# Block-sparse attention and a leaky MLP in one kernel: the weights' sign from ScalarE's multiplication, attention in bursts of four units, new priorities

## The chip, the core and the metric

The kernel runs on one core of a Trainium2 chip. The metric is the device time of one execution in microseconds; a smaller one is better. TensorE (PE in the profile) multiplies matrices, VectorE (DVE), ScalarE (ACT) and GpSimd (POOL) do elementwise work, and SyncE (SP) issues the loads and stores.

## The reference

Four sequences of 768 positions with 8 heads of 64 go through attention in which a query sees the keys less than 16 positions away and the 24 block summaries of its head (maximum of keys, mean of values, over blocks of 32). The result, 3072 rows of 512, goes through two matrix products with a leaky step between them:

```
k_sum = k.reshape(B, H, nb, 32, D).max(axis=3); v_sum = v.reshape(B, H, nb, 32, D).mean(axis=3)
scores_l = where(|pos_q - pos_k| < 16, scale * q @ k.T, -1e9);  scores_s = scale * q @ k_sum.T + log(32)
a = softmax(concat(scores_l, scores_s));  x = a @ concat(v, v_sum)      # then heads side by side
h = x @ w_in;  g = maximum(0.01 * h, h);  out = g @ w_out               # (3072,512) (512,2048) (2048,512)
```

## The kernel before

**The MLP.** The rows are cut into 8 chunks of 384 (`T`), and the 2048 middle columns into 16 steps `f` of 128. Each operand is split into a high and a low part in fp32r, and a product is three: high by high, high by low, low by high. For a chunk and a step, `m1` puts 12 matmuls of 384 columns into a PSUM tile `h` (an "h block"); ScalarE makes `ghi` and `gs` from it (L538, L535), the leaky step in high part and in full; VectorE subtracts them to `glo` (L541); `m2` adds 9 matmuls of 512 columns (an "a block", L550 to L552) into three accumulators. An a block stands behind the h block of the next step. The order of the parts is chunk 0 with the first `SPL` steps, chunk 1 with all, the rest of chunk 0, and then chunk by chunk, so that the weights may come in little by little.

**Weights.** w_in and w_out stay in SBUF. `weights(f, w, t)` prepares a block of 128 by 512 for each step and matrix, 32 in all. The words arrive as float64 (`raw`, in a ring of 6 buffers tagged "big"), each as two 32-bit words, and are put together to float32: s0 shifts the low word right by 29 (VectorE, L485), s1 copies the sign as a 16-bit mask from the high word (VectorE, L489), s2 multiplies the high word, read as a float32, by 2^-112, which moves the exponent (ScalarE, L492), s3 shifts it left by 3 and joins the two (VectorE, L495), s4 makes the high part (ScalarE, L498), s5 the low part by subtraction (VectorE, L501).

**Attention.** A unit is 128 queries of a pair of heads, 12 units to a chunk, 96 in all. `pair(m)` handles two units in three pieces on TensorE: "s" (scores, L323, 8 matmuls that the trace shows as 16 rows), "t" (4 transposes of the normalized exponentials, L340), and "o" (values, L346, 8 matmuls, 16 rows). Between s and t VectorE takes mask and maximum (L328), ScalarE the exponential (L335), VectorE the norm (L408, L412, L416); between t and o ScalarE copies the transposes (`pt`, L426); behind o ScalarE and VectorE write x in two parts (L435, L438). From chunk 1 on, `group` joins the scores of one pair, the values of the second pair before it and the transposes of the one between them to a group on TensorE, which stands among the MLP's blocks.

**What sets the order.** Every operation is given to a list scheduler (`Plan`) with an engine, a cost and a priority; `order` runs through a model of the engines, the load queue and the buffers and writes down a fixed order for each engine. The constants at the head of the file (`PLACE`, `OFF`, `LOADS`, `PL`, `WT` and others) are priorities in units of attention. On TensorE, "spare" matmuls on zeros (L639) are put in up to the first h block where the plan expects it to wait.

Of the kernel before, what the change touches and what calls it, by code (L numbers as in the profile page):

```python
# [8 lines left out]
F32 = mybir.dt.float32  # L9
# [15 lines left out]
LK = 120  # L25
TPC = 3
# [16 lines left out]
PL = -1.087
WS = 0.974
WS2 = 1.452
LD = 4.616
XP = 0.547
VT = 2.875
KP = -0.231
KS = -2.395  # L50
XW = -1.124
B1 = 6
USQ = 0.579
WT = 3.757
W0 = 0.79
WO = 1.464
CUT = 3
OFF = {'s': (1.446, 0.604), 'ttr': (-4.554, 0.093), 'ex': (1.991, -0.067), 'nrm': (-1.17, 0.313), 't': (-2.49, -0.132), 'pt': (-3.602, 1.198), 'o': (2.219, -0.005), 'xhi': (0.869, -0.883), 'xlo': (10.088, -1.826)}
LOADS = [('kn', 0, 1), ('q', 0, 0), ('kn', 0, 0), ('q', 0, 1), ('vb', 0, 0), ('mask',), ('vb', 0, 2), ('kn', 0, 2), ('vb', 0, 1), ('kn', 0, 3), ('q', 0, 3), ('q', 0, 2), ('v', 0, 2), ('v', 0, 0), ('v', 0, 1), ('w', 0, 0), ('v', 0, 3), ('w', 1, 0), ('w', 1, 1), ('w', 0, 1)]
# [91 lines left out]
def build(tc, ctx, a):  # L151
# [201 lines left out]
    def group(m, phase, kind, cost, fn, **kw):  # L353
        j = m + "sto".index(kind)
# [24 lines left out]
        return x["op"], g  # L379

    def pair(m):
# [74 lines left out]
        o = pe("t", 600, v1, tr, [("a0", kt, 1)], after=[nm], use=[("e", m)])  # L456
        o = P.op("ACT", ACT(512, True), v1 + 0.3 + off("pt"), pt, after=[o], use=[kt], alloc=[(tag_p, ("pt", m), buf_p)])
        o = pe("o", 600, v2, av, [(ko_tag, ko, 1)], after=[o] + v_op[c, p] + v_op[c, p1], use=[("pt", m)] + kv)
# [8 lines left out]
    def weights(f, w, t):  # L467
# [34 lines left out]
        o = load_op(("w", f, w), t - 0.25 * BIG, load, alloc=[("big", kr, BIG)], size=128 * 4096, rate=290.0)  # L502
        o = P.op("DVE", DVE(512, True), t + 0.05, s0, after=[o], use=[kr], port=True)
# [16 lines left out]
    def mlp(c, f0, f1, t0):  # L520
# [16 lines left out]
        def ghi(f):  # L537
            nc.scalar.activation(out=gnew("ghi", G("ghi", f)), in_=tl[G("h", f)][:, :T], func=AF.Prelu, alpha=0.01)  # L538
# [154 lines left out]
```

## Time and profile before

| | |
|---|---|
| median of three runs | 656.93 us (656.62 to 657.16) |
| span of the profiled execution | 654.36 us; its own time is not listed, and the median lies 2.57 us above the span |
| TensorE busy | 643.2 us (98%), 4613 matmul rows |
| VectorE busy | 280.5 us (43%), nearly all of the first 120 us |
| ScalarE busy | 294.4 us (45%) |
| loads and stores | 58.07 MB |

A row of an engine gives the start and the duration of an instruction in the span. TensorE's instructions overlap and their ends are modelled, so what a block costs is read from its start to the start of what follows.

### The profile page before, as it was taken

Reading aid. Unit: us, or ns where it says so; the run is one execution under the profiler, and the core shown is the slowest. Engines: PE = TensorE matmul, PEld = TensorE weight load, DVE = VectorE, ACT = ScalarE, POOL = GpSimd, SP = SyncE. Lnnn points to the kernel's source line nnn. Section 1 sums busy time; section 2 is a strip of 40 time slices with the busy share of each in tenths; the row PEclk is TensorE's granted clock in tenths of the full one; section 3 lists DMA queues with packets and bytes.
Section 4 is the critical chain, followed back from the end, with each engine's and each line's share of the span. In section 5 each row is a group of like instructions: output and inputs, shape, how many; then the busy total and the mean of one; then the engine's idle time right before and its main releaser. Section 6 shows DMA issues by size and latency. Waiting matters only on the chain.

```text
span 654.4 us, 11674 instructions
## 1 busy us (share of the span) xinstructions
PE 643.2 (98%) x4613; PEld 561.7 (86%) x4613; DVE 280.5 (43%) x907; ACT 294.4 (45%) x874; POOL 6.9 (1%) x18
## 2 busy tenths in 40 slices
PE   8899999999999999999999999999999999999997
PEld 6687788889888888888888898888888988899996
DVE  5899999741475333322534242233223322111111
ACT  4798777353554433534434353354334433222112
POOL 2100000000000000000000000000000000000000
PEclk9999999999999999999999999999999999999999
DMA  8987775500464111121613021121001200010001
GB/s 303 288 251 224 226 233 184 162 26 14 137 189 136 54 43 46 38 72 36 179 51 112 24 72 37 36 83 37 13 24 48 72 1 2 0 50 1 0 1 48
DMA packets 27206, 58.07 MB, mean 89 GB/s; under 512 B 3024, under 2 KB 13328, under 8 KB 27152
## 3 DMA queue, kind: packets, MB, share of 16 engines
q1 hardware_dynamic: 27152, 57.33, 28.7%
q8 instruction: 36, 0.59, 0.4%
q14 instruction: 18, 0.15, 0.1%
HBM read 48.97 MB, written 6.29 MB: 84 GB/s over the span
## 4 chain that ended last, share of the span: by engine, by line
PE 84%; DVE 14%; ACT 1%; issue 1%; ACTq 0%
PE h L531 36%; PE a L552 12%; PE a L551 12%; PE a L550 12%; DVE raw L489 3%; DVE raw L495 2%; DVE win_lo L501 2%; DVE raw L485 1%; DVE wout_lo L501 1%; PE spare L639 1%; DVE glo L541 1%; DVE e L328 1%; DVE e L416 1%; ACT e L335 1%; DVE xl L438 1%
## 5 line engine op out<-in xcount | busy, mean ns | idle before, releaser
L541 DVE TENSOR_TENSOR glo<-gs,ghi 128x384 fp32r<-128x384 f32 x128 | 71.4, 558 | 265.9 <-ACT gs L535 264.0
L531 PE MATMUL h<-xh,win_hi 128*128 128x384 f32 x512 | 175.7, 343 | 0.4 <-ACT win_hi L498 0.4
L538 ACT ACTIVATE ghi<-h 128x384 fp32r<-128x384 f32 x128 | 62.7, 490 | 251.1 <-PE h L531 250.9
L531 PE MATMUL h<-xh,win_lo 128*128 128x384 f32 x512 | 173.6, 339 | 0.3 <-DVE win_lo L501 0.2
L531 PE MATMUL h<-xl,win_hi 128*128 128x384 f32 x512 | 173.2, 338 | 0.0
L552 PE MATMUL a<-wout_hi,glo 128*128 128x512 f32 x384 | 151.7, 395 | 0.9 <-DVE glo L541 0.8
L551 PE MATMUL a<-wout_lo,ghi 128*128 128x512 f32 x384 | 150.8, 393 | 1.5 <-DVE wout_lo L501 1.5
L550 PE MATMUL a<-wout_hi,ghi 128*128 128x512 f32 x384 | 151.8, 395 | 0.0
L531 PEld LDWEIGHTS h<-xh,win_hi 128*128 128x128 f32 x512 | 96.1, 188 | 5.2 <-ACT win_hi L498 1.1
L531 PEld LDWEIGHTS h<-xl,win_hi 128*128 128x128 f32 x512 | 96.4, 188 | 4.4
L531 PEld LDWEIGHTS h<-xh,win_lo 128*128 128x128 f32 x512 | 96.1, 188 | 1.4 <-DVE win_lo L501 1.4
L552 PEld LDWEIGHTS a<-wout_hi,glo 128*128 128x128 f32 x384 | 72.1, 188 | 17.8 <-DVE glo L541 2.5
L551 PEld LDWEIGHTS a<-wout_lo,ghi 128*128 128x128 f32 x384 | 72.2, 188 | 13.8 <-DVE wout_lo L501 2.5
L550 PEld LDWEIGHTS a<-wout_hi,ghi 128*128 128x128 f32 x384 | 72.1, 188 | 11.0 <-issue 0.2
L335 ACT ACTIVATE e<-e,m 128x120 f32<-128x120 f32 x192 | 73.7, 389 | 9.6 <-DVE m L328 9.6
L535 ACT ACTIVATE gs<-h 128x384 f32<-128x384 f32 x128 | 62.3, 487 | 0.2 <-DVE glo L541 0.2
L335 ACT ACTIVATION_READ_ACCUMULATOR e<-e,m 128x1 f32 x192 | 36.7, 191 | 0.0
L416 DVE TENSOR_TENSOR e<-e,z 128x480 f32<-128x480 f32 x48 | 32.1, 669 | 1.3
L492 ACT ACTIVATE raw<-raw 128x512 f32<-128x512 f32 x32 | 21.8, 693 | 10.4 <-DVE raw L489 9.5
L408 DVE TENSOR_SCALAR z<-z 128x4 f32<-128x4 f32 x48 | 8.2, 172 | 36.6 <-ACT e L335 36.5
L489 DVE TENSOR_SCALAR raw<-raw 128x512 int16<-128x512 int16 x32 | 23.4, 766 | 0.0
L495 DVE SCALAR_TENSOR_TENSOR raw<-raw 128x512 int32<-128x512 int32 x32 | 21.6, 694 | 0.0
(588 smaller groups left out, 520.3 us busy)
## 6 DMA issues: line engine op xcount, KB each, us to landing
raw<-in_w_dram SPq DMA_DIRECT2D x32, 512.0 KB
v<-in_v_dram SPq DMA_DIRECT2D x32, 288.0 KB
kn<-in_k_dram SPq DMA_DIRECT2D x16, 400.0 KB
k<-in_q_dram SPq DMA_DIRECT2D x32, 192.0 KB
out_dram<-out SPq DMA_DIRECT2D x21, 256.0 KB
vb<-in_vb_dram SPq DMA_DIRECT2D x12, 384.0 KB
kn<-in_k_dram SPq DMA_DIRECT2D x16, 208.0 KB
v<-vsum SPq DMA_DIRECT2D x24, 72.0 KB
```

The source lines that it names most:

```text
L335: nc.scalar.activation(out=e[:, n], in_=e[:, n], func=AF.Exp, scale=-1.0, bias=m[:, n:n + 1], accum_out=z[:, n:n + 1])
L416: nc.vector.tensor_tensor(out=e, in0=e, in1=z.unsqueeze(2).broadcast_to([128, 4, LK]), op=ALU.mult)
L489: nc.vector.tensor_scalar(out=w16[:, :, 1], in0=w16[:, :, 3], scalar1=-2 ** 15, scalar2=None, op0=ALU.bitwise_and)
L492: nc.scalar.mul(hw(), hw(), 2.0 ** -112)
L495: nc.vector.scalar_tensor_tensor(out=li(), in0=hi_i(), scalar=3, in1=li(), op0=ALU.logical_shift_left, op1=ALU.bitwise_or)
L531: nc.tensor.matmul(h[:, :T], w[:, k, 128 * f:128 * f + 128], x[:, k], start=n == 0, stop=n == 11)
L535: nc.scalar.activation(out=new("gs", G("gs", f), [128, T], bufs=1), in_=tl[G("h", f)][:, :T], func=AF.Prelu, alpha=0.01)
L538: nc.scalar.activation(out=gnew("ghi", G("ghi", f)), in_=tl[G("h", f)][:, :T], func=AF.Prelu, alpha=0.01)
L541: nc.vector.tensor_tensor(out=gnew("glo", G("glo", f)), in0=tl[G("gs", f)], in1=tl[G("ghi", f)].bitcast(F32), op=ALU.subtract)
L550: nc.tensor.matmul(o, gh, wout_hi[:, f], start=f == f0, stop=False)
L551: nc.tensor.matmul(o, gh, wout_lo[:, f], start=False, stop=False)
L552: nc.tensor.matmul(o, gl, wout_hi[:, f], start=False, stop=f == f1 - 1)
```

## The change

Three edits.

1. In `weights`, s1 is taken out. s2 becomes the leaky step `Prelu` with scale 2^-112 and slope 2^32 for negative words: a negative word leaves it with an exponent 32 higher, and behind the shift left by 3 that bit is the sign. s2 follows the load directly and no longer s1; s3 waits for s0 and s2.
2. From chunk 2 on, `quad(q)` replaces `pair(m)`: the scores of four units in one block, with the transposes of a pair before; then the values of the four units before, in one block, with other transposes. x is written in 512 columns at a time. The number and sizes of the matmuls stay. Chunks 0 and 1 keep pairs.
3. The costs of the pieces in the plan and all priorities are set anew; `SPL` is 11 instead of 10, and `CUT`, the number of steps whose h block is cut in two at the start, 1 instead of 3. gs and ghi get priorities of their own, and gs now stands ahead of ghi.

```diff
-        def s1():
-            w16 = tl[kr].bitcast(I16).rearrange("p (n t) -> p n t", t=4)
-            nc.vector.tensor_scalar(out=w16[:, :, 1], in0=w16[:, :, 3], scalar1=-2 ** 15, scalar2=None, op0=ALU.bitwise_and)
-
         def s2():
-            nc.scalar.mul(hw(), hw(), 2.0 ** -112)
+            nc.scalar.activation(out=hw(), in_=hw(), func=AF.Prelu, scale=2.0 ** -112, alpha=2.0 ** 32)
...
-        o = P.op("DVE", DVE(512, True), t + 0.1, s1, after=[o], use=[kr], port=True)
-        o = P.op("ACT", ACT(512), t + 0.1, s2, after=[o], use=[kr])
-        o = P.op("DVE", DVE(512), t + 0.12, s3, after=[o], use=[kr], port=True)
+        o1 = P.op("ACT", ACT(512), t + 0.05, s2, after=[lo_], use=[kr])
+        o = P.op("DVE", DVE(512), t + 0.12, s3, after=[o, o1], use=[kr], port=True)
...
+    def quad(q):
+        us = range(4 * q, 4 * q + 4)
...
+        def qk():
+            for n, u in enumerate(us):
+                scores(u, [tl[ks[0]], tl[ks[1]]], LK * n)
...
+        def av():
+            for n, u in enumerate(us):
+                values(u, tl[ko], 128 * n)
...
+        s_op = group(2 * q, 2, "s", CS4, qk, after=[o for p in hs for o in k_op[c, p]], use=[("k", c, p) for p in hs])[0]
...
+            kt = ("to", ("g", 2 * q + 1 + w, 2))
+            o = group(2 * q + 1 + w, 2, "t", CT, lambda m=m, kt=kt: tr(m, kt), after=o, use=[("e", m)])[0]
...
+        o = group(2 * q + 3, 2, "o", CO4, av, after=pts + [o for p in hs for o in v_op[c, p]], use=[("pt", 2 * q), ("pt", 2 * q + 1)] + [("v", c, p) for p in hs])[0]
...
-    for m in range(NCH * UPC // 2):
+    for m in range(2 * UPC // 2):
         pair(m)
+    for q in range(2 * UPC // 4, NCH * UPC // 4):
+        quad(q)
```

TensorE's order in the even stretch, a group of chunk 6 among the blocks of chunk 5; `s_('g', ...)` is the PSUM tile of scores and values, `to_('g', ...)` that of transposes. Before:

```order
L552 MATMUL a_0_2_4089<-wout_hi,glo_8_4440 128x512
L323 MATMUL s_('g', 36, 2)_4470<-k_0_4265 64x120 x2
L323 MATMUL s_('g', 36, 2)_4471<-k_0_4265 64x120 x2
L323 MATMUL s_('g', 36, 2)_4470<-k_0_4265 64x120 x2
L323 MATMUL s_('g', 36, 2)_4471<-k_0_4265 64x120 x2
L346 MATMUL s_('g', 36, 2)_4470<-pt_4396,v_2_3891 64x64 x4
L346 MATMUL s_('g', 36, 2)_4470<-pt_4396,v_3_4137 64x64 x4
L340 MATMUL to_('g', 36, 2)_4472<-ident,e_4392 120x128 x4
L531 MATMUL h_10_4493<-xh_80,win_hi 128x384
```

In the changed kernel, the group of the same number and the next one:

```order
L610 MATMUL a_0_2_4061<-wout_hi,glo_8_4394 128x512
L323 MATMUL s_('g', 36, 2)_4424<-k_0_4222 64x120 x2
...
L323 MATMUL s_('g', 36, 2)_4425<-k_1_4236 64x120 x2
L340 MATMUL to_('g', 36, 2)_4426<-ident,e_4226 120x128 x4
L589 MATMUL h_10_4447<-xh_80,win_hi 128x384
...
L610 MATMUL a_0_2_4061<-wout_hi,glo_11_4536 128x512
L346 MATMUL s_('g', 37, 2)_4566<-pt_4364,v_2_3867 64x64 x4
L346 MATMUL s_('g', 37, 2)_4566<-pt_4364,v_3_4108 64x64 x4
L346 MATMUL s_('g', 37, 2)_4566<-pt_4462,v_3_4108 64x64 x8
L340 MATMUL to_('g', 37, 2)_4567<-ident,e_4468 120x128 x4
L589 MATMUL h_13_4588<-xh_80,win_hi 128x384
```

A group holds two kinds instead of three, and each of s and o has twice as many matmuls in a row. By the whole of the order there are, behind the first h block, 44 groups before, and 45 in the changed kernel: 18 s and 18 o of double length, 5 s, 6 o and 42 t of the old one.

VectorE's order in the ramp, where the blocks of w_out and w_in of one step (`raw_1_780`, `raw_0_824`) are prepared. Before:

```order
L485 TENSOR_SCALAR raw_0_824<-raw_0_824 128x512
L408 TENSOR_SCALAR z_915<-z_915 128x4
L485 TENSOR_SCALAR raw_1_834<-raw_1_834 128x512
L412 RECIPROCAL z_915<-z_915 128x4
L489 TENSOR_SCALAR raw_0_824<-raw_0_824 128x512
L416 TENSOR_TENSOR e_913<-e_913,z_915 128x480
L495 SCALAR_TENSOR_TENSOR raw_1_780<-raw_1_780 128x512
L495 SCALAR_TENSOR_TENSOR raw_0_824<-raw_0_824 128x512
L541 TENSOR_TENSOR glo_3_970<-gs_3_948,ghi_3_941 128x384
L489 TENSOR_SCALAR raw_1_834<-raw_1_834 128x512
L485 TENSOR_SCALAR raw_0_886<-raw_0_886 128x512
L501 TENSOR_TENSOR wout_lo<-raw_1_780,wout_hi 128x512
```

In the changed kernel, one step later:

```order
L560 TENSOR_TENSOR win_lo<-raw_0_861,win_hi 128x4x128
L599 TENSOR_TENSOR glo_4_1025<-gs_4_1019,ghi_4_1022 128x384
L548 TENSOR_SCALAR raw_1_917<-raw_1_917 128x512
L554 SCALAR_TENSOR_TENSOR raw_1_917<-raw_1_917 128x512
L554 SCALAR_TENSOR_TENSOR raw_0_876<-raw_0_876 128x512
L599 TENSOR_TENSOR glo_5_1062<-gs_5_1056,ghi_5_1059 128x384
L548 TENSOR_SCALAR raw_1_966<-raw_1_966 128x512
L560 TENSOR_TENSOR wout_lo<-raw_1_917,wout_hi 128x512
```

Between shift (L548) and join (L554) the 16-bit instruction is gone, and the join may follow the shift at once.

ScalarE's order around the exponentials of a pair before, in the even stretch:

```order
L426 COPY pt_4888<-to_('g', 39, 2)_4847 120x512
L335 ACTIVATE e_4884,z_4886<-e_4884,m_4885 128x120 x4
L538 ACTIVATE ghi_2_4907<-h_2_4868 128x384
L535 ACTIVATE gs_2_4911<-h_2_4868 128x384
L538 ACTIVATE ghi_3_4939<-h_3_4917 128x384
```

and around those of a burst in the changed kernel:

```order
L490 COPY pt_4462<-to_('g', 36, 2)_4426 120x512
L335 ACTIVATE e_4464,z_4466<-e_4464,m_4465 128x120 x4
L335 ACTIVATE e_4468,z_4470<-e_4468,m_4469 128x120
L593 ACTIVATE gs_10_4494<-h_10_4447 128x384
L596 ACTIVATE ghi_10_4497<-h_10_4447 128x384
L335 ACTIVATE e_4468,z_4470<-e_4468,m_4469 128x120 x3
```

Five exponentials stand ahead of gs and ghi instead of four, and three behind them.

## Rows read from the trace of the kernel before

**Rows 1.** Stretches: busy us of PE, PEld, DVE, ACT, POOL; clock, DMA share, GB/s.
```profile
20.00:40.00 20.00, 17.83 (x295) 14.77 (x287) 19.13 (x80) 17.82 (x64) 2.63 (x4) 1.00 0.89 278
40.00:60.00 20.00, 18.78 (x146) 14.99 (x143) 19.94 (x57) 17.59 (x47) 0.00 (x0) 1.00 0.67 215
60.00:80.00 20.00, 19.04 (x134) 15.77 (x133) 20.00 (x57) 16.10 (x42) 0.00 (x0) 1.00 0.76 240
...
100.00:120.00 20.00, 19.36 (x95) 16.57 (x93) 20.00 (x36) 13.65 (x28) 0.00 (x0) 1.00 0.67 205
120.00:140.00 20.00, 20.00 (x128) 17.68 (x128) 9.40 (x23) 5.79 (x18) 0.00 (x0) 1.00 0.27 69
```
**Rows 2.** Waits of TensorE: us in total, times, the longest.
```profile
PE a L551 <- DVE wout_lo L501: 1.5, 3, 0.6
```

**Rows 3.** Timeline of TensorE (start, duration): first h block, two a blocks of the tail.
```profile
34.09 0.42 PE L531 MATMUL h<-xh,win_hi 128*128 128x384 f32 x1
...
570.91 0.39 PE L550 MATMUL a<-wout_hi,ghi 128*128 128x512 f32 x1
...
646.21 0.39 PE L550 MATMUL a<-wout_hi,ghi 128*128 128x512 f32 x1
```

**Rows 4.** Timeline of TensorE around a group: first rows of h, s, o, t, a, h.
```profile
161.00 0.34 PE L531 MATMUL h<-xh,win_hi 128*128 128x384 f32 x1
...
163.19 0.32 PE L323 MATMUL s_('g', 15, 2)_2043<-k 64*64 64x120 f32 x2
...
163.76 0.69 PE L346 MATMUL s_('g', 15, 2)_2043<-pt,v 120*64 120x64 f32 x16
164.38 0.65 PE L340 MATMUL to_('g', 15, 2)_2045<-ident,e 128*120 128x128 f32 x4
164.79 0.47 PE L550 MATMUL a<-wout_hi,ghi 128*128 128x512 f32 x1
...
166.94 0.34 PE L531 MATMUL h<-xh,win_hi 128*128 128x384 f32 x1
```

**Rows 5.** Timeline of TensorE at the start: fillers, scores of two pairs in one block.
```profile
19.20 0.50 PE L639 MATMUL spare<-zero 128*128 128x128 bf16 x6
19.63 1.05 PE L323 MATMUL s<-k 64*64 64x120 f32 x32
20.61 0.28 PE L639 MATMUL spare<-zero 128*128 128x128 bf16 x2
```

**Rows 6.** Groups by line and form: values of a pair (busy us, mean ns).
```profile
L346 PE MATMUL s_('g', 12, 1)_1197<-pt,v 120*64 120x64 f32 x16 | 0.7, 228 | 0.0
```

**Rows 7.** Timeline of TensorE: values straight behind an h block, transposes, an a block.
```profile
75.72 0.69 PE L346 MATMUL s_('g', 12, 1)_1197<-pt,v 120*64 120x64 f32 x16
76.33 0.66 PE L340 MATMUL to_('g', 12, 1)_1198<-ident,e 128*120 128x128 f32 x4
76.75 0.48 PE L550 MATMUL a<-wout_hi,ghi 128*128 128x512 f32 x1
```

**Rows 8.** Groups by line, VectorE and ScalarE: busy us, mean ns, idle time before.
```profile
L489 DVE TENSOR_SCALAR raw<-raw 128x512 int16<-128x512 int16 x32 | 23.4, 766 | 0.0
...
L335 ACT ACTIVATE e<-e,m 128x120 f32<-128x120 f32 x192 | 73.7, 389 | 9.6 <-DVE m L328 9.6
L538 ACT ACTIVATE ghi<-h 128x384 fp32r<-128x384 f32 x128 | 62.7, 490 | 251.1 <-PE h L531 250.9
...
L492 ACT ACTIVATE raw<-raw 128x512 f32<-128x512 f32 x32 | 21.8, 693 | 10.4 <-DVE raw L489 9.5 <-ACT e L335 0.8
```

**Rows 9.** Timeline of VectorE: the sign step and what follows it.
```profile
40.27 0.76 DVE L489 TENSOR_SCALAR raw<-raw 128x512 int16<-128x512 int16 x1
40.81 0.60 DVE L541 TENSOR_TENSOR glo<-gs,ghi 128x384 fp32r<-128x384 f32 x1
```

**Rows 10.** Timelines of VectorE and TensorE: a glo, and the matmul that needs it.
```profile
155.84 0.56 DVE L541 TENSOR_TENSOR glo<-gs,ghi 128x384 fp32r<-128x384 f32 x1 [3.61 <-ACT gs L535]
...
159.39 0.39 PE L552 MATMUL a<-wout_hi,glo 128*128 128x512 f32 x1
```

More of the change, by code (lines that the diff above doesn't have):

```diff
@@ L34 @@
 KR, VR, PTR, ER = 2, 3, 2, 2
+CS, CT, CO, CS4, CO4, Q2, PQ = 590, 520, 640, 1000, 1110, -1.008, -13.431
 FGAP, WARM = 300, 5500
-SPL = 10
-PARTS = [(0, 0, SPL), (1, 0, NF), (0, SPL, NF)] + [(c, 0, NF) for c in range(2, NCH)]
+SPL = 11
 XB = [0, 1] + [(c + 1) % 2 for c in range(2, NCH)]
-PLACE = {0: (0.0, 1.0), 1: (12.43, 0.579), 2: (31.69, 0.2), 3: (38.07, 0.839)}
+PLACE = {0: (-0.427, 0.524), 1: (13.237, 0.656), 2: (29.792, 0.277), 3: (37.406, 0.574)}
 BACC = {"dynamic_dma_scratch_size": 1024}
[L43 to L59, printed above, removed]
+PL = -6.456
+WS = 0.842
+WS2 = 3.261
+LD = 4.734
+XP = 3.922
+VT = 0.047
+KP = -0.85
+KS = -7.385
+XW = 1.224
+B1 = 1.206
+GH, GS, GL, GM = -2.579, -5.801, -3.881, 1.289
+WT = 2.051
+W0 = -1.714
+WO = 1.478
+CUT = 1
+OFF = {'s': (1.021, 0.681), 'ttr': (-4.813, 0.259), 'ex': (3.429, 0.028), 'nrm': (0.069, 0.916), 't': (0.683, -0.137), 'pt': (-7.577, 1.142), 'o': (1.396, 0.242), 'xhi': (3.796, -1.282), 'xlo': (10.172, -1.893)}
+LOADS = [('kn', 0, 1), ('q', 0, 0), ('kn', 0, 0), ('mask',), ('q', 0, 1), ('vb', 0, 0), ('vb', 0, 1), ('kn', 0, 3), ('vb', 0, 2), ('q', 0, 3), ('kn', 0, 2), ('q', 0, 2), ('v', 0, 1), ('v', 0, 0), ('w', 0, 0), ('v', 0, 2), ('v', 0, 3), ('w', 1, 0), ('w', 0, 1), ('w', 1, 1)]
 class Plan:
@@ L350, in x_of, with group @@
         return x[XB[c]].rearrange("p a t -> p (a t)")[:, 128 * r:128 * r + n]
-    def group(m, phase, kind, cost, fn, **kw):
-        j = m + "sto".index(kind)
+    def group(j, phase, kind, cost, fn, **kw):
         g = ("g", j, phase)
@@ L441, in pe @@
             if c:
-                return group(m, ph, kind, cost, fn, **kw)[0]
+                return group(m + "sto".index(kind), ph, kind, cost, fn, **kw)[0]
             return P.op("PE", cost, prio + off(kind), fn, alloc=alloc, **kw)
-        o = pe("s", 758, v + 0.1, qk, [("h", ks[0], 2), ("h", ks[1], 2)] if wide else [("s0", ks[0], 1), ("s1", ks[1], 1)], after=k_op[c, p] + k_op[c, p1], use=kk)
+        o = pe("s", CS, v + 0.1, qk, [("h", ks[0], 2), ("h", ks[1], 2)] if wide else [("s0", ks[0], 1), ("s1", ks[1], 1)], after=k_op[c, p] + k_op[c, p1], use=kk)
         e, z = [], []
@@ L455, in pair @@
         nm = P.op("DVE", DVE(4 * LK), v + 0.55 + off("nrm"), nrm, after=[rc], use=[("e", m), ("z", m)], port=True)
[L456 removed]
+        o = pe("t", CT, v1, tr, [("a0", kt, 1)], after=[nm], use=[("e", m)])
         o = P.op("ACT", ACT(512, True), v1 + 0.3 + off("pt"), pt, after=[o], use=[kt], alloc=[(tag_p, ("pt", m), buf_p)])
[L458 removed]
+        o = pe("o", CO, v2, av, [(ko_tag, ko, 1)], after=[o] + v_op[c, p] + v_op[c, p1], use=[("pt", m)] + kv)
         al = [(f"x{XB[c]}", ("x", c), 1)] if r == 0 else []
@@ L461, in pair, with norm, tr, pt @@
         o2 = P.op("DVE", DVE(256), v2 + 0.35 - XP + off("xlo"), xlo, after=[o1], use=[ko, ("x", c)])
+        x_op.setdefault(c, []).extend([o1, o2])
+    def quad(q):
+        us = range(4 * q, 4 * q + 4)
+        c, r = where(4 * q)[:2]
+        hs = sorted({where(u)[2] for u in us})
+        v = place(4 * q)
+        gs, go = ("g", 2 * q, 2), ("g", 2 * q + 3, 2)
+        ks, ko = [("s0", gs), ("s1", gs)], ("s0", go)
+        def qk():
+            for n, u in enumerate(us):
+                scores(u, [tl[ks[0]], tl[ks[1]]], LK * n)
+        def norm(m, n):
+            e, _, z = tiles_of(m)
+            if n == 0:
+                nc.vector.tensor_scalar(out=z, in0=z, scalar1=1e-9, scalar2=None, op0=ALU.add)
+            elif n == 1:
+                nc.vector.reciprocal(out=z, in_=z)
+            else:
+                nc.vector.tensor_tensor(out=e, in0=e, in1=z.unsqueeze(2).broadcast_to([128, 4, LK]), op=ALU.mult)
+        def tr(m, kt):
+            for n in range(2):
+                turn(2 * m + n, tl[kt], 256 * n)
+        def pt(m, kt):
+            new("pt", ("pt", m), [128, 512], bufs=PTR)
+            nc.scalar.copy(tl["pt", m].rearrange("p (h q) -> p h q", h=4)[:LK], tl[kt][:LK].rearrange("p (h q) -> p h q", h=4))
+        def av():
+            for n, u in enumerate(us):
+                values(u, tl[ko], 128 * n)
+        def xhi():
+            nc.scalar.copy(x_of(xh, c, r, 512), tl[ko])
+        def xlo():
+            nc.vector.tensor_tensor(out=x_of(xl, c, r, 512), in0=tl[ko], in1=x_of(xh, c, r, 512).bitcast(F32), op=ALU.subtract)
+        s_op = group(2 * q, 2, "s", CS4, qk, after=[o for p in hs for o in k_op[c, p]], use=[("k", c, p) for p in hs])[0]
+        pts = []
+        for w in range(2):
+            m = 2 * q + w
+            b = v + Q2 * w
+            e, z = [], []
+            for n in range(2):
+                for h in range(2):
+                    al = [(x, (x, m), ER) for x in "emz"] if h + n == 0 else []
+                    col = LK * (2 * w + n)
+                    z.append(P.op("DVE", 205, b + 0.2 + 0.1 * n, lambda u=2 * m + n, h=h, col=col: lowest(u, h, tl[ks[h]][:, col:col + LK]),
+                                  after=[s_op] + z[:1], use=[ks[h], ("e", m), ("m", m)], alloc=al))
+                    e.append(P.op("ACT", ACT(LK, extra=2), b + 0.3 + 0.1 * n, lambda u=2 * m + n, h=h: expo(u, h), after=z[-1:], use=[("e", m), ("m", m), ("z", m)]))
+            o = e
+            for n in range(3):
+                o = [P.op("DVE", DVE(4 * LK) if n == 2 else 70, b + 0.45 + 0.05 * n, lambda m=m, n=n: norm(m, n), after=o, use=[("z", m)] + [("e", m)] * (n == 2), port=True)]
+            kt = ("to", ("g", 2 * q + 1 + w, 2))
+            o = group(2 * q + 1 + w, 2, "t", CT, lambda m=m, kt=kt: tr(m, kt), after=o, use=[("e", m)])[0]
+            pts.append(P.op("ACT", ACT(512, True), place(4 * q + 2 + 2 * w) + 0.3 + PQ, lambda m=m, kt=kt: pt(m, kt), after=[o], use=[kt], alloc=[("pt", ("pt", m), PTR)]))
+        o = group(2 * q + 3, 2, "o", CO4, av, after=pts + [o for p in hs for o in v_op[c, p]], use=[("pt", 2 * q), ("pt", 2 * q + 1)] + [("v", c, p) for p in hs])[0]
+        al = [(f"x{XB[c]}", ("x", c), 1)] if r == 0 else []
+        o1 = P.op("ACT", ACT(512, True), place(4 * q + 6) + 0.3 + PQ, xhi, after=[o] + ([x_op[c][0]] if r else []), use=[ko, ("x", c)], alloc=al)
+        o2 = P.op("DVE", DVE(512), place(4 * q + 6) + 0.35 + PQ - XP, xlo, after=[o1], use=[ko, ("x", c)])
@@ L501, in s5 @@
             nc.vector.tensor_tensor(out=lo, in0=shape(lw()), in1=hi.bitcast(F32), op=ALU.subtract)
-        o = load_op(("w", f, w), t - 0.25 * BIG, load, alloc=[("big", kr, BIG)], size=128 * 4096, rate=290.0)
-        o = P.op("DVE", DVE(512, True), t + 0.05, s0, after=[o], use=[kr], port=True)
-        o = P.op("DVE", DVE(512, True), t + 0.1, s1, after=[o], use=[kr], port=True)
-        o = P.op("ACT", ACT(512), t + 0.1, s2, after=[o], use=[kr])
-        o = P.op("DVE", DVE(512), t + 0.12, s3, after=[o], use=[kr], port=True)
+        lo_ = load_op(("w", f, w), t - 0.25 * BIG, load, alloc=[("big", kr, BIG)], size=128 * 4096, rate=290.0)
+        o = P.op("DVE", DVE(512, True), t + 0.05, s0, after=[lo_], use=[kr], port=True)
+        o1 = P.op("ACT", ACT(512), t + 0.05, s2, after=[lo_], use=[kr])
+        o = P.op("DVE", DVE(512), t + 0.12, s3, after=[o, o1], use=[kr], port=True)
         o = P.op("ACT", ACT(512), t + 0.3, s4, after=[o], use=[kr])
@@ L617, in build @@
             weights(f, w, LEAD - WT + min(f, SPL) * WS + max(f - SPL, 0) * WS2 + WO * w + (W0 if f == 0 else 0))
-    for m in range(NCH * UPC // 2):
+    for m in range(2 * UPC // 2):
         pair(m)
+    for q in range(2 * UPC // 4, NCH * UPC // 4):
+        quad(q)
     t = LEAD
-    for c, f0, f1 in PARTS:
+    for c, f0, f1 in [(0, 0, SPL), (1, 0, NF), (0, SPL, NF)] + [(c, 0, NF) for c in range(2, NCH)]:
         mlp(c, f0, f1, t)
```

14 lines of the change are left out of this document (7 added, 7 removed).

## Prediction, made before the changed kernel ran

> **What bounds the kernel now.** I read the table of stretches first [rows 1]. Up to 120 us VectorE is busy in every microsecond (19.94 to 20.00 of 20) while TensorE has small holes (18.78, 19.04 and 19.36 of 20); from 120 us on VectorE falls to 9.40 and TensorE is full, 20.00 of 20, at a granted clock of 1.00. So there are two regimes: a ramp in which VectorE prepares weights too slowly, and after it a long stretch in which nothing but TensorE's own work counts. The waits of TensorE [rows 2] name what is late in the ramp: the low halves of w_out, VectorE's last step on a weight.
>
> The holes are larger than the idle column says, since a matmul's end is modelled and overhangs the next start; I therefore count from start to start. Between two blocks of the tail without attention, 570.91 and 646.21 us, lie 18 steps f [rows 3], so a step costs 75.30/18 = 4.183 us. An attention group costs what stands between its starts [rows 4]: scores 0.57 (163.19 to 163.76), values 0.62, transposes 0.41, and the two changes around it: the h block ahead takes 2.19 and the a block behind 2.15, together 0.16 more than the 4.183 of a plain step (I use 0.17, with rounding).
>
> From the first h (34.09) to the last a block (646.21) pass 612.1 us [rows 3]. Work in it: 126 whole steps and two h blocks, 527.1 + 4.2 = 531.3; by the order, 40 scores, 42 values and 41 transposes in 44 groups, 22.8 + 26.0 + 16.8 + 7.5 = 73.1. That is 604.4, so **TensorE waits 7.7 us** in the ramp. Ahead of it lie 34.1 us of start, behind it 8.15 us of ending (654.36 - 646.21), which the change leaves alone. The span is 654.36 us, and the median of the three runs, 656.93, is 2.57 above it; I add the same 2.57 to my span.
>
> **The bursts of four.** Number and size of matmuls stay; a group of scores, values and transposes becomes two kinds, scores of four units with transposes, and values of four units with transposes. Eighteen bursts replace 36 pairs. Sixteen score rows cost 0.57; thirty-two in one block cost 0.98 (19.63 to 20.61) [rows 5]. So the second half adds only 0.41, and 0.16 of the 0.57 belongs to the change of kind. For values the trace has no double block: one row of 228 ns [rows 6] inside a block of 0.69 puts the 16 starts (0.69 - 0.23)/15 = 0.031 apart, so a second half adds 0.49 and a double block costs 1.11, 0.13 saved. The new neighbours exist already: a group with values straight behind h costs 0.61 and 0.42 [rows 7], no dearer than behind scores. Sum: 18 x (0.16 + 0.13) = 5.2 off, one group more (45 for 44) 0.17 on: **-5.05 us**. Bounds: nothing saved (+0.2), or values saving as scores do (-5.6). I take the value from the rows, as the score row is the same instruction.
>
> The row says that a block has a price of its own and a matmul in it little. The Trainium skill (TensorEngine Tiling (Array Packing), section Key Properties) states that a change of tiling mode drains TensorE, and these three kinds are tiled 64x64, 128x64 and 128x128; by that the saving stands, and the trace agrees with 0.98 against twice 0.57. The same page (section Instruction Overhead) speaks against it: it puts some 60 cycles on each matmul, and as their number is unchanged the bursts would save nothing by that alone. The double score block is against this reading.
>
> **The sign on ScalarE.** The 16-bit step that copied the sign goes from VectorE: 32 instructions with a mean of 766 ns [rows 8], but the next one starts 0.54 after it (40.27 to 40.81) [rows 9], so 32 x 0.54 = 17.3 us of VectorE time. On ScalarE the multiplication becomes a leaky step on the same 512 elements: the old one took 693, the leaky step on 384 elements from h takes 490 [rows 8]; scaled up by columns that is 653. I cost it at nothing; if it were 10% dearer, 32 x 0.07 = 2.2 us of an engine that is busy 16 to 18 of 20 us [rows 1]. The step also no longer waits for VectorE's sign; both start from the landed load, and s3 waits for both.
>
> VectorE is full from 40 to 120 us, and TensorE lost 7.7 us to it. Taking 17.3 us out is more than twice the loss, so VectorE stops being the bound and the pace becomes TensorE's step. What is late next: ScalarE, which had 17.59 of 20 in 40 to 60 and carries the same work in a shorter ramp, and the loads, which run at 205 to 240 GB/s there while the first stretch shown reached 278 [rows 1], so they have room. I leave two to four waits of the present kind, 2.5 us: **-5.2 us** (bounds: 0, if ScalarE takes VectorE's place in full, and -7.7).
>
> **The new priorities at the start.** They move three things. On SP's queue the mask goes ahead of the second block of queries, one load of 0.2 MB ahead of another, and nothing waits on SP for either. By the order, the first h now stands ahead of the last pair's scores and transposes (0.57 + 0.41), which run behind it: +0.98 behind the start, the same off ahead of it. And w_in's first block is loaded earlier, while 33 filler matmuls stand where 6 stood ahead of the scores of the fourth and fifth pair. A filler costs 0.43/6 = 0.072 [rows 5], so if they are not covered by the wait for keys and queries those scores come (33 - 6) x 0.072 = 1.9 us later; if they are, nothing. From these scores (19.63) to the first h (34.09) before lie 14.46 us [rows 3, 5], with, by the order, three sign steps on VectorE (1.6 us) and the 0.98 in it; VectorE is full there (19.13 of 20), but ScalarE too (17.82), so only part comes out. I put the first h at 33.6: -0.5, with bounds -2.5 and +1.5. With the 0.98 that is **+0.5 us**.
>
> **The dense and the even stretch.** In the even stretch, a glo ends at 156.40 and the matmul that needs it starts at 159.39 [rows 10]: 3.0 us of slack. A burst sets four or five exponentials (389 ns each [rows 8]) ahead of gs and ghi, 1.9 us, and the order lets the other three stand behind them. This cover holds in the sum. A burst also reads two key tiles, all there are, so the next load of queries, and ScalarE's copy of keys behind it, wait until its scores are done; three bursts to 16 steps put the next one 5.3 x 4.183 = 22 us later, and a late copy has that time. Copies of x in 512 columns for two of 256 take less of ScalarE and VectorE, off the path. In the dense stretch, where the second batch's first chunks are fed, one or two places have scores of a burst one a block (2.1 us) behind values of another, with the same PSUM tile; I count that within the 2.5.
>
> **Sum.** -5.05 - 5.2 + 0.5 = -9.75: span 644.6, time **647.2 us**, 1.5% less.
>
> **Rivals.** (A) ScalarE or the loads hold the weights, so that the waits stay: 5.2 lost, 652.4. For it: ScalarE's 17.6 of 20. Against it: its busy share falls to 13.65 by 100 to 120 us while VectorE stays at 20.00, and the waits shown name VectorE. (B) The bursts save nothing, that is a block's price grows with its matmuls: 5.1 lost, 652.3; against it stands the block of 0.98. (C) Better: fillers covered, the first h at 32.0, and 0.5 us of waits: 3.6 less, 643.6. (D) Slower: the bursts make glo late. If the eight reductions, the norm and the exponentials of a burst push gs back by more than the 3.0 us, each burst stalls TensorE; 656.93 x 1.002 = 658.2 is reached at 11 us over my time, 0.61 us for each of 18 bursts, so glo must come 3.6 us later than now. The order speaks against it, since gs and ghi stand inside the burst's exponentials, and from 120 to 140 us VectorE is busy 9.40 and ScalarE 5.79 of 20. The Trainium skill (Perfetto Trace Analysis, section Tensor Engine Instruction) says that ScalarE and VectorE take their instructions strictly in order, which is why such a block could hold gs at all; no row here shows one overtaking. (E) Several small losses together, 655.6 to 658.2, which cannot be told from no change: 0.2% of 656.93, 1.3 us, is about what a measurement of this kernel can tell.
>
> **Chances.** Forecast (645 to 650.5) 0.60, A 0.13, B 0.07, C 0.10, D 0.05, E 0.05. The range 643.0 to 653.0 takes in the forecast, most of A, B and C, and leaves D, E and some of the mishaps that add up, 0.2 in all. Faster by over 0.2%: 0.90; within: 0.05; slower: 0.05.
>
> **What would show it.** Right: VectorE below 18 of 20 in 60 to 120 us; TensorE's waits for w_out's low half gone or halved; double score blocks of 0.98 and value blocks of 1.11 between starts; first h near 33.6; from 130 us on no wait. Wrong: value blocks at 1.24; waits of a or h blocks on ScalarE's weight halves; a first h beyond 35; a wait for glo or for a PSUM tile at each burst.

## The result, and the profile after

The changed kernel takes **644.67 us** (median of four runs, 644.53 to 644.97); the kernel before, on the same chip, 657.04 (656.62 to 657.17). The ratio is 0.9814, with a 95% interval of 0.980 to 0.983. The forecast was 647.2 us. The profiled execution has a span of 642.7 us at a granted clock of 1.00.

The same stretches as in [rows 1], with the same columns:

```profile
20.00:40.00 20.00, 18.80 (x295) 15.72 (x293) 17.45 (x75) 17.83 (x64) 2.73 (x3) 1.00 0.98 291
40.00:60.00 20.00, 20.00 (x155) 17.06 (x153) 18.63 (x55) 18.39 (x50) 0.00 (x0) 1.00 0.83 254
60.00:80.00 20.00, 20.00 (x170) 17.42 (x170) 19.75 (x56) 19.16 (x49) 0.00 (x0) 1.00 0.84 268
80.00:100.00 20.00, 19.77 (x113) 17.73 (x112) 19.29 (x33) 12.82 (x29) 0.00 (x0) 1.00 0.98 275
100.00:120.00 20.00, 20.00 (x128) 17.80 (x127) 11.27 (x27) 9.03 (x20) 0.00 (x0) 1.00 0.29 96
```

TensorE is full from 40 us on but for 0.2 us, yet VectorE is not idle: it stays at 19.75 and 19.29 of 20 until 100 us and falls only then, one stretch earlier than before. The weights are prepared in a shorter ramp, at 254 to 275 GB/s where it was 205 to 240. The waits of TensorE say what the busy share does not. This is the whole list; the one of the kernel before, from which [rows 2] shows the longest, had 3.2 us of waits behind its first h:

```profile
PE spare L699 <- DVE zero L691: 1.0, 1, 1.0
PE t L340 <- ACT e L335: 0.5, 1, 0.5
PE t L340 <- DVE k L282: 0.4, 2, 0.2
PE s_('g', 13, 1)_1322 L346 <- DVE xl L437: 0.2, 1, 0.2
```

The first three lie ahead of the first h; in the ramp 0.2 us is left by this list. On TensorE's timeline (start, duration), the first h and the first a block, a scores burst with its neighbours, a values burst, and the last a block, beside [rows 3, 4]:

```profile
33.22 0.42 PE L589 MATMUL h<-xh,win_hi 128*128 128x384 f32 x1
...
39.43 0.39 PE L608 MATMUL a<-wout_hi,ghi 128*128 128x512 f32 x1
...
160.63 0.32 PE L323 MATMUL s_('g', 16, 2)_2084<-k 64*64 64x120 f32 x2
...
161.61 0.65 PE L340 MATMUL to_('g', 16, 2)_2086<-ident,e 128*120 128x128 f32 x4
162.02 0.42 PE L589 MATMUL h<-xh,win_hi 128*128 128x384 f32 x1
...
168.50 1.15 PE L346 MATMUL s_('g', 17, 2)_2196<-pt,v 120*64 120x64 f32 x32
169.59 0.65 PE L340 MATMUL to_('g', 17, 2)_2197<-ident,e 128*120 128x128 f32 x4
169.99 0.48 PE L608 MATMUL a<-wout_hi,ghi 128*128 128x512 f32 x1
...
634.56 0.39 PE L608 MATMUL a<-wout_hi,ghi 128*128 128x512 f32 x1
```

From start to start, a double score block costs 0.98 and a double value block 1.09 (1.08 in the mean of 18). From the first h to the last a block pass 601.34 us, where 612.12 passed before. The leaky step in the groups by line, beside [rows 8], and, beside [rows 10], a glo in the middle of a burst with the matmul that needs it:

```profile
L551 ACT ACTIVATE raw<-raw 128x512 f32<-128x512 f32 x32 | 21.1, 693 | 0.5 <-DMA raw<-in_w_dram 0.5
```
```profile
167.09 0.53 DVE L599 TENSOR_TENSOR glo<-gs,ghi 128x384 fp32r<-128x384 f32 x1
```
```profile
170.55 0.39 PE L610 MATMUL a<-wout_hi,glo 128*128 128x512 f32 x1
```

The leaky step takes 693 ns, exactly what the multiplication took, and ScalarE's 9.5 us of waiting for the sign are gone. The glo ends at 167.62, 2.9 us ahead of its matmul. Over all glos from 130 us on, the very last one aside, the smallest such slack is 2.65 us, and it was 2.60 before: the bursts don't press on it.

### The profile page after: what moved, and what is told of

Same layout as the page of the kernel before. It is cut to its first block, busy times and chain, and to the rows that moved or that the text cites. A ratio compares the mean times of both kernels' runs of the same rounds, so it can differ in the third digit from the quotient of the medians.

```text
span 642.7 us, 11789 instructions
## 1 busy us (share of the span) xinstructions
PE 636.2 (99%) x4634; PEld 561.4 (87%) x4634; DVE 265.8 (41%) x857; ACT 290.0 (45%) x856; POOL 7.9 (1%) x18
## 4 chain that ended last, share of the span: by engine, by line
PE 91%; DVE 3%; ACT 2%; issue 0%; ACTq 0%
PE h L589 41%; PE a L610 13%; PE a L609 13%; PE a L608 13%; ACT e L335 1%; DVE raw L554 1%; DVE wout_lo L560 0%; DVE raw L548 0%; DVE win_lo L560 0%; ACT win_hi L557 0%; DVE e L328 0%; PE spare L699 0%; ACT pt L425 0%; ACT xh L434 0%; DVE xl L437 0%
## 5 line engine op out<-in xcount | busy, mean ns | idle before, releaser
L482 DVE TENSOR_TENSOR e<-e,z 128x480 f32<-128x480 f32 x36 | 23.7, 658 | 1.2
L554 DVE SCALAR_TENSOR_TENSOR raw<-raw 128x512 int32<-128x512 int32 x32 | 21.7, 688 | 1.0 <-ACT raw L551 0.2
L267 ACT COPY k<-kn 128x288 f32<-128x288 f32 x56 | 20.9, 436 | 1.1 <-DMA kn<-in_k_dram 1.1
L200 DVE TENSOR_REDUCE ksum<-kn 128x24 f32<-128x768 f32 x16 | 15.2, 948 | 7.0 <-DMA kn<-in_k_dram 7.0
```

The lines of the kernel that those rows point to most:

```text
L267: nc.scalar.copy(k, x) if c else nc.gpsimd.tensor_copy(k, x)
L482: nc.vector.tensor_tensor(out=e, in0=e, in1=z.unsqueeze(2).broadcast_to([128, 4, LK]), op=ALU.mult)
```

## The experiments

The theory: two effects that add up. A change of kind on TensorE (a block of scores, values or transposes next to a block of another kind) has a price of its own, which the bursts save; and VectorE's time set the ramp, which the sign's move frees. Rivals: the price is per matmul (B); the new priorities did it; what counted was a weight's longer chain; ScalarE or the loads hold the ramp (A).

Differences to the changed kernel are differences of medians from several chips, on which the kernel before took 656.63 to 657.04 us, so a few tenths of a microsecond say nothing. A ratio is always to the kernel before on the same chip. The prediction's count of waits (the time from the first h to the last a block, less 531.3 us of steps, the attention blocks and 0.17 for each group) is used again for the experiments.

**Each edit undone, and both (E1 to E3).** E1 takes the bursts away:

```
-    for m in range(2 * UPC // 2):
+    for m in range(NCH * UPC // 2):
         pair(m)
-    for q in range(2 * UPC // 4, NCH * UPC // 4):
-        quad(q)
```

> The changed kernel with its bursts of four undone: from the third chunk on pairs again, 44 attention groups in place of 45; the sign on ScalarE and the new priorities stay. Theory (each change of kind has a price of its own): 18 x (0.16 + 0.15) less one group of 0.17, some 5.4 us come back, so 650 us (649 to 651.5), with the first h block and the waits of the ramp as in the changed kernel. Rival B (the price is per matmul): 644.7 us, no change.

Measured: 650.87 us (650.03 to 651.32; ratio to before 0.991, 0.9896 to 0.9923), 6.2 above the changed kernel. Its two ends on TensorE's timeline:

```profile
33.50 0.42 PE L589 MATMUL h<-xh,win_hi 128*128 128x384 f32 x1
...
640.75 0.39 PE L608 MATMUL a<-wout_hi,ghi 128*128 128x512 f32 x1
```

Between them lie 607.25 us, 5.9 more than in the changed kernel. The attention blocks alone, from start to start, add up to 66.4 us in E1 and 60.7 in the changed kernel, with the same 45 groups (the expectation had 44): 5.7 of the 5.9. The waits stay, 1.9 us by the count as against 1.7. Rival B foresaw no change.

E2 puts the sign step back:

```
+        def s1():
+            w16 = tl[kr].bitcast(I16).rearrange("p (n t) -> p n t", t=4)
+            nc.vector.tensor_scalar(out=w16[:, :, 1], in0=w16[:, :, 3], scalar1=-2 ** 15, scalar2=None, op0=ALU.bitwise_and)
...
-            nc.scalar.activation(out=hw(), in_=hw(), func=AF.Prelu, scale=2.0 ** -112, alpha=2.0 ** 32)
+            nc.scalar.mul(hw(), hw(), 2.0 ** -112)
...
-        o1 = P.op("ACT", ACT(512), t + 0.05, s2, after=[lo_], use=[kr])
-        o = P.op("DVE", DVE(512), t + 0.12, s3, after=[o, o1], use=[kr], port=True)
...
+        o = P.op("DVE", DVE(512, True), t + 0.1, s1, after=[o], use=[kr], port=True)
+        o = P.op("ACT", ACT(512), t + 0.1, s2, after=[o], use=[kr])
+        o = P.op("DVE", DVE(512), t + 0.12, s3, after=[o], use=[kr], port=True)
```

> The changed kernel with the 16-bit sign step back on VectorE and the plain multiplication on ScalarE; bursts and priorities stay. Theory (VectorE's 17.3 us set the pace of the ramp): the waits of TensorE go from about 1.2 back to 6 to 8 us, so 649.5 to 652 us, VectorE at 19.9 of 20 up to 115 us or later, the waits on the low halves of w_out back. Rival (the new priorities took the waits away, and the sign's place is nothing): 644.7 to 646 us.

Measured: 651.01 us (650.70 to 651.55; ratio 0.9914, 0.990 to 0.9928), 6.3 above the changed kernel. Its first h stands at 34.34, 1.1 later, and between it and the last a block lie 606.43 us, 5.1 more, with 6.8 us of waits by the count:

```profile
34.34 0.42 PE L594 MATMUL h<-xh,win_hi 128*128 128x384 f32 x1
...
640.77 0.39 PE L613 MATMUL a<-wout_hi,ghi 128*128 128x512 f32 x1
```

TensorE's longest waits, and the stretches of the ramp:

```profile
PE a L614 <- DVE wout_lo L564: 2.1, 5, 0.5
PE a L613 <- ACT wout_hi L561: 1.1, 1, 1.1
```
```profile
60.00:80.00 20.00, 19.33 (x164) 16.03 (x163) 19.93 (x56) 15.85 (x41) 0.00 (x0) 1.00 0.78 250
80.00:100.00 20.00, 19.08 (x107) 16.48 (x106) 20.00 (x39) 14.57 (x29) 0.00 (x0) 1.00 0.72 221
100.00:120.00 20.00, 19.89 (x100) 17.64 (x99) 19.55 (x34) 10.56 (x22) 0.00 (x0) 1.00 0.80 227
```

The picture of before is back: VectorE full to 120 us, w_out's low halves late, and ScalarE waiting for the sign. From 40 to 118 us ScalarE's rescaling waited 8.0 us for the sign step:

```profile
L555 ACT ACTIVATE raw<-raw 128x512 f32<-128x512 f32 x24 | 16.2, 692 | 8.9 <-DVE raw L552 8.0 <-ACT e L335 0.6 <-DVE z L411 0.2
```

E3 makes both edits of E1 and E2; only the new priorities are left.

> The changed kernel with both edits undone, so that of the change only the new table of priorities is left. Theory (the two edits bring all, and add up): 655 to 657.5 us, that is the changed kernel plus the loss of e1 plus the loss of e2. Rival (the priorities bring a part of their own): 653 us or less. Second rival (the edits help only each other): e1's and e2's losses do not add up to this one's.

Measured: 657.45 us (656.87 to 658.17; ratio 1.0011, 1.0002 to 1.002). The losses of E1 and E2 add up to 12.5, and E3's is 12.8: under the new priorities the two effects are independent. The new priorities without the edits bring nothing, rather a loss of 0.7.

**The sign alone under the old priorities (E4).** The kernel before with E2's lines turned round.

> The kernel before with the sign on ScalarE alone; pairs and the old priorities stay. Theory (VectorE's time in the ramp is what counts, whatever the priorities): the waits fall from 7.7 to 1 to 3 us, so 650.5 to 652.5 us. Rival A (ScalarE or the loads take VectorE's place): 656 to 657 us. Rival (the weights' due times must be set anew for it): 654 to 657 us.

Measured: 652.37 us (652.03 to 652.51; ratio 0.9933, 0.992 to 0.9945), 4.3 below before, inside the theory's range; by the count 3.7 us of waits are left, more than the 1 to 3 expected. E1 differs from it by the third edit alone and is 1.5 faster; the two intervals just touch. One wait stands out:

```profile
PE h L526 <- ACT gs L530: 2.1, 1, 2.1
```

So the new priorities bring nothing while VectorE holds everything back (E3), and some 1.5 us once it does not. Bursts alone under the old priorities weren't tried.

**Changes of kind doubled, matmuls unchanged (E5).** In the groups of the bursts:

```
-                for y in "sot":
-                    if y in x:
-                        x[y]()
+                if g[2] == 2:
+                    for w in range(2):
+                        for y in "sot":
+                            if y in x:
+                                x[y](w)
+                else:
+                    for y in "sot":
+                        if y in x:
+                            x[y]()
...
```

> The changed kernel with the same matmuls, but in each of the 34 groups of a burst with transposes the order alternates: half of the scores (or values), two transposes, the other half, two transposes. So two changes of kind more per group and not one matmul more. Theory (a change of kind has a price): two score blocks of 0.57 for one of 0.98, two value blocks of 0.62 for one of 1.08, and two blocks of transposes for one of 0.41: 0.16 to 0.3 per group, 5.4 to 10 us in all, so 650 to 655 us. Rival B (the price is per matmul): 644.7 us, no change.

Measured: 655.31 us (654.61 to 655.51; ratio 0.9974, 0.9965 to 0.9983), 10.6 above the changed kernel and a little above the theory's range. One group on the timeline, from its first scores to the h behind it:

```profile
161.70 0.32 PE L323 MATMUL s_('g', 16, 2)_2084<-k 64*64 64x120 f32 x2
...
162.28 0.43 PE L340 MATMUL to_('g', 16, 2)_2086<-ident,e 128*120 128x128 f32 x2
162.64 0.32 PE L323 MATMUL s_('g', 16, 2)_2084<-k 64*64 64x120 f32 x2
...
163.21 0.43 PE L340 MATMUL to_('g', 16, 2)_2086<-ident,e 128*120 128x128 f32 x2
163.40 0.42 PE L594 MATMUL h<-xh,win_hi 128*128 128x384 f32 x1
```

It takes 1.70 us from start to start (0.58, 0.36, 0.57, 0.19) where the same matmuls took 1.39 (0.98 and 0.41, above). All attention blocks together take 70.98 us as against 60.74: 10.2 of the 10.6 (the first h stands 0.46 later in this execution). With 68 changes of kind added, one costs 0.15 us. Rival B is out. Both kinds bear it: the scores together take 1.15 for 0.98, and the transposes 0.55 for 0.41, 0.36 of it in the half ahead of scores and 0.19 in the half ahead of h.

**Fewer fillers at the start (E6 to E8).** Ahead of the scores at 20.24 us stand 33 fillers; the forecast left open whether they delay anything. The edit, for E6, E7 and E8 with 900, 1500 and 2300:

```
-FGAP, WARM = 300, 5500
+FGAP, WARM = 900, 5500
```

> The changed kernel with fewer fillers at the start (they fill a planned gap up to 0.9 us before its end, in place of 0.3). Theory (the 33 fillers ahead of the fourth pair's scores run on after the keys are there and delay the chain to the first h): those scores, at 20.24, come up to 0.6 us earlier and the first h, at 33.22, up to 0.6 us earlier: 644.1 to 644.7 us. Rival (the fillers lie under VectorE's and ScalarE's chain): 644.7 us. Second rival (TensorE's granted clock falls with fewer fillers): above 645 us, with a granted clock below 1.00 before the first h.

> As the run before, with the fill ending 1.5 us before the planned end of a gap. Theory (fillers delay the chain): the fourth pair's scores up to 1.2 us earlier, 643.5 to 644.5 us. Rival (they lie under VectorE's and ScalarE's chain): 644.7 us. Second rival (granted clock falls): above 645 us.

> As the two runs before, with the fill ending 2.3 us before the planned end of a gap; nearly all fillers between the pairs go. Theory (fillers delay the chain): the fourth pair's scores as early as their keys, some 1.9 us earlier, and the first h up to that: 642.8 to 644.2 us. Rival (hidden): 644.7 us. Second rival (granted clock falls): above 646 us, with stretches below 1.00 before the first h.

Measured: 644.21 (644.04 to 644.29; ratio 0.9806, 0.9793 to 0.9819), 643.89 (643.31 to 644.51; 0.9802, 0.9788 to 0.9815) and 645.48 us (642.97 to 645.91; 0.9818, 0.9801 to 0.9836). The intervals of all three ratios overlap that of the changed kernel, so a gain of 0.5 to 0.8 us for E6 and E7 is not resolved; E8's median lies outside what the theory and both rivals expected of it. In E6 the first h did come 1.2 us earlier, more than the 0.6 that the theory allowed, but the first a block only 0.3 (39.43 in the changed kernel), with a wait for the first weights in between:

```profile
32.02 0.45 PE L589 MATMUL h<-xh,win_hi 128*128 128x384 f32 x1
...
39.14 0.39 PE L608 MATMUL a<-wout_hi,ghi 128*128 128x512 f32 x1
```
```profile
PE h L589 <- ACT win_hi L557: 0.4, 1, 0.4
```

In E7 and E8 the clock fell as well, and the first h, at 33.34 and 33.62, came no earlier than in the changed kernel. Stretches of 4 us of E7, with the columns of [rows 1]:

```profile
24.00:28.00 4.00, 2.14 (x39) 1.71 (x38) 3.94 (x17) 4.00 (x16) 0.22 (x1) 1.00 0.87 286
28.00:32.00 4.00, 2.58 (x30) 1.97 (x32) 2.48 (x13) 3.52 (x9) 0.00 (x0) 0.53 0.94 279
32.00:36.00 4.00, 4.00 (x41) 3.63 (x41) 3.89 (x16) 3.23 (x12) 0.00 (x0) 0.62 0.84 281
```

What the clock costs shows from execution to execution: four of E8's five had a mean granted clock of 0.989 to 0.991 and took 645.14 to 645.91 us, the fifth had 1.000 and took 642.97. So the fillers take up to 1.7 us with one hand (by that one execution) and hold the clock with the other, which is worth 2 to 3; what is left is small.

**What in the sign step counted (E9).** E2 brought back VectorE's time and a link in each weight's chain together. E9 brings back the time alone, a step that changes nothing and that ScalarE does not wait for:

```
+        def s1():
+            w16 = tl[kr].bitcast(I16).rearrange("p (n t) -> p n t", t=4)
+            nc.vector.tensor_scalar(out=w16[:, :, 1], in0=w16[:, :, 1], scalar1=-1, scalar2=None, op0=ALU.bitwise_and)
...
+        o = P.op("DVE", DVE(512, True), t + 0.1, s1, after=[o], use=[kr], port=True)
```

> The changed kernel, sign on ScalarE as it is, with a 16-bit step of the same shape and the same cost put back on VectorE for each of the 32 weights, that changes nothing and for which ScalarE does not wait. In e2 the step came back on VectorE and into the chain of a weight at once (ScalarE waited 8.0 us for it); here only VectorE's time comes back. Theory (VectorE's time sets the ramp): about e2's loss, 649.5 to 651.5 us. Rival (the chain's length, load to sign to rescaling, was what counted): 644.7 to 646 us.

Measured: 651.50 us (650.94 to 652.34; ratio 0.992, 0.9905 to 0.9935), as E2 and at the upper end of the theory's range; the count gives 7.6 us of waits. Three of TensorE's waits in the ramp, put down to VectorE's e and to weight halves:

```profile
PE to_('g', 7, 1)_717 L340 <- DVE e L415: 1.2, 1, 1.2
PE to_('g', 12, 1)_1268 L340 <- ACT win_hi L561: 1.2, 1, 1.2
PE a L614 <- DVE wout_lo L564: 1.1, 2, 0.8
```

VectorE's time alone brings the whole loss; that ScalarE waits for the sign adds nothing that these runs resolve.

**VectorE lighter still, ScalarE heavier (E10, E11).** E10 takes one more step of each weight from VectorE:

```
-            nc.vector.scalar_tensor_tensor(out=li(), in0=hi_i(), scalar=3, in1=li(), op0=ALU.logical_shift_left, op1=ALU.bitwise_or)
+            nc.vector.tensor_scalar(out=li(), in0=hi_i(), scalar1=3, scalar2=None, op0=ALU.logical_shift_left)
...
-        o = P.op("DVE", DVE(512, True), t + 0.05, s0, after=[lo_], use=[kr], port=True)
+        o = lo_
```

> The changed kernel with one more step taken from VectorE: the shift of the low word (32 times 422 ns) goes, and the joining step only shifts; so the three lowest bits of each weight are left out. VectorE still had 19.3 to 19.8 of 20 us busy from 60 to 100 us in the changed kernel. Theory (TensorE's own pace is the bound of the ramp now, its waits are about 1.2 us, and at the start the loads hold): 643.5 to 644.7 us, at most 1.2 us. Rival (VectorE, as full as it reads, still holds the ramp and the start): 641 to 643 us.

Measured: 643.96 us (643.66 to 644.12; ratio 0.9803, 0.9789 to 0.9818). VectorE went down by 2.9 and 3.6 of 20 in these two stretches, and the time by 0.7, which is not resolved. The loads moved 300 GB/s in the first of them, where the changed kernel's moved 268, so in that stretch they had room as well:

```profile
60.00:80.00 20.00, 20.00 (x181) 17.07 (x182) 16.87 (x49) 19.56 (x50) 0.00 (x0) 1.00 0.91 300
80.00:100.00 20.00, 20.00 (x102) 18.27 (x103) 15.73 (x26) 11.89 (x27) 0.00 (x0) 1.00 0.93 243
```

E11 adds a copy on ScalarE to each weight:

```
             nc.scalar.activation(out=hw(), in_=hw(), func=AF.Prelu, scale=2.0 ** -112, alpha=2.0 ** 32)
+            nc.scalar.copy(hw(), hw())
```

> The changed kernel with a second ScalarE instruction of 512 elements in each weight (a copy onto itself behind the leaky step), 32 times 0.69 us = 22 us more of ScalarE, in the chain too. ScalarE has 18.4 and 19.2 of 20 us busy in 40 to 80 us. Theory (ScalarE is the next bound, with about 1 us of room in 20): TensorE's waits come to what before had on VectorE or more, 650 to 662 us, with weight halves named as ScalarE's. Rival (ScalarE is busy early because it may run ahead, and has room): under 648 us.

Measured: 659.91 us (659.24 to 661.18; ratio 1.0053, 1.0037 to 1.007), 15.2 above the changed kernel for 22 us of ScalarE (21 if counted from start to start). TensorE's two longest waits and the stretches:

```profile
PE s_('g', 13, 1)_1345 L346 <- DVE xl L437: 3.4, 1, 3.4
PE a L609 <- ACT wout_hi L558: 3.1, 3, 1.7
```
```profile
60.00:80.00 20.00, 18.44 (x139) 15.63 (x138) 15.52 (x47) 19.74 (x49) 0.00 (x0) 0.91 0.72 225
80.00:100.00 20.00, 15.79 (x96) 12.77 (x95) 17.10 (x42) 19.51 (x43) 0.00 (x0) 0.91 0.68 211
```

The second wait is for weight halves, as expected. The longest is not: it is for an xl of VectorE, which itself stood behind ScalarE's copy of x (xh, at 94.02), with ScalarE busy on weights for 3.94 of the 4 us around it. So ScalarE's backlog held up attention too.

ScalarE would be the next bound, with some 6 to 9 us of room over the ramp. This is an estimate: 21 - 15.2 is 6, and up to 3.6 of the 15.2 are TensorE's lower clock (0.91 over these 40 us). The copy also makes a weight's chain longer, and E11 does not tell the two apart. Rival A's mechanism is real, but the change did not use up ScalarE's room.

## Why the prediction was right, point by point

The forecast's mechanisms held, and the time lay inside its range, 2.5 us under the likeliest value. The terms all missed on the same side, so no errors cancelled. Each term by its own accounts:

- **Bursts: -5.05 forecast, some -5.7 measured.** The double score block was right at 0.98. The value block was put at 1.11 from the spacing of starts and is 1.08, so it saves 0.15 and not 0.13; 18 x (0.16 + 0.15) = 5.6, and E1 gives 5.7. The group more that the forecast charged with 0.17 is not the bursts': E1 and E3, without them, have 45 groups too, so it comes with the new priorities.
- **Waits in the ramp: -5.2 forecast, -6.0 measured.** By the forecast's own count the changed kernel has 531.3 of steps, 60.7 of attention blocks and 45 x 0.17 = 7.7 of edges in its 601.34 us, so 1.7 us of waits are left, from 7.7; the forecast left 2.5. E2 and E9 bring 6.8 and 7.6 us of waits back, so the sign step's time on VectorE was the cause.
- **Start: +0.5 forecast, +0.1 measured.** The first h came 0.9 earlier (34.09 to 33.22) where 0.5 was forecast, against the same 0.98 moved behind it. One execution can't tell the two apart: E1 and E5 have the same blocks up to the first h as the changed kernel, and theirs stand at 33.50 and 33.68. The sign's share is 0.5 to 1.1 us, by E2 (34.34) and E9 (34.22) against these three. The fillers were not free, but most of what they delayed was covered by the first weights (E6).
- **The profiled execution against the median.** The sum gives -11.6, and the span fell by 11.7. The forecast added 2.57 us to its span; for this kernel it is 644.67 - 642.7 = 2.0. In every execution listed the time is 1.7 to 1.9 us above its own span, so the profiled execution of the kernel before was 0.7 or more below the median, and the forecast set the one against the other. The misses are 0.65, 0.8, 0.4 and 0.6: together the 2.5.
- **ScalarE's step at nothing: right**, 693 ns before and after.
- **The even stretch: right.** No wait of TensorE after 130 us is listed, and glo's slack hardly moved; rival D is out.

One sign that was named did not show: VectorE was to fall below 18 of 20 from 60 to 120 us, and stayed at 19.75 and 19.29 until 100. That step failed in its logic, though not in its result. Taking work from VectorE didn't make it idle; it made it finish earlier, by 100 us instead of 120. E10 shows that its full row is no longer a bound. Rival A, at 0.13, was nearer than the forecast argued: a falling busy share late in the ramp said little of the room in 40 to 80 us, which E11 measures.

The Trainium skill (TensorEngine Tiling (Array Packing), section Key Properties) has a change of tiling mode drain TensorE; E5 agrees, with 0.15 us for each change added, though no row here shows that it is a drain. The same page of the Trainium skill (section Instruction Overhead) puts some 60 cycles on each matmul; by that alone an unchanged number of matmuls would have cost the same, which misses the 10.6 us of E5.

## What to carry to other kernels

Price a small block of matmuls from two block sizes in the trace: the part that doesn't grow with the block belongs to the change of kind, and merging blocks saves it. Before relieving an engine that reads as full, look at what waits for it, and judge afterwards by the waits and by when its work ends, not by its busy share, which can stay full. Ask at once which engine is next and how many microseconds of room it has; here it was an estimated 6 to 9 us on ScalarE, about half of what VectorE gave up or less.

## What the runs showed of the hardware that was not expected

The price of a change of kind depends on which kinds meet: two transposes ahead of an h block cost 0.19, the same two ahead of scores 0.36 (E5). Part of the difference comes back in the h block, which costs 2.20 behind transposes as against 2.11 behind an a block, so 0.09.

With fewer fillers TensorE was busy 2.14 of 4 us from 24 to 28 us (E7), and in the next two stretches the granted clock was 0.53 and 0.62, close to the lower level of 1.2 GHz, though in the second of them TensorE was busy all the time. In the changed kernel, busy 3.4 of 4 us from 24 to 28 with the fillers' help, it stayed at 1.00:

```profile
24.00:28.00 4.00, 3.43 (x59) 2.87 (x60) 3.85 (x17) 4.00 (x15) 0.90 (x1) 1.00 0.88 262
```

E11 shows the same in mid-kernel, behind a hole of TensorE from 92 to 95 us:

```profile
92.00:96.00 4.00, 1.08 (x17) 0.97 (x17) 3.60 (x8) 3.94 (x9) 0.00 (x0) 0.89 0.62 189
96.00:100.00 4.00, 4.00 (x14) 3.33 (x15) 3.27 (x7) 3.94 (x9) 0.00 (x0) 0.69 1.00 294
100.00:104.00 4.00, 4.00 (x22) 3.61 (x21) 3.62 (x7) 3.17 (x7) 0.00 (x0) 1.00 0.91 224
```

```profile
97.31 0.63 PE L609 MATMUL a<-wout_hi,ghi 128*128 128x512 f32 x1
97.74 0.63 PE L610 MATMUL a<-wout_lo,ghi 128*128 128x512 f32 x1
```

Busy for all of the second stretch, TensorE had a clock of 0.69 there. The matmuls of an a block start 0.43 us apart in it, as against 0.23 in the next stretch at 1.00 (102.07 and 102.30): here a starved TensorE paid for its wait a second time.
